# Retention, GLU and ReLU² in one kernel: v is scaled behind the state copy in the lone stage, conversions stand behind a pair's outputs, raw pieces are requested one by one, and k, v go ahead of the GLU blocks

## The chip, the core and the metric

The kernel runs on one core of a Trainium2 chip. The metric is the device time of the whole program in microseconds, the median over runs. The engines are TensorE (PE in the profile, PEld for its weight loads), VectorE (DVE), ScalarE (ACT), GpSimd (POOL) and SyncE (SP), which here only issues DMA requests. Each engine works through its own instructions in the order in which they were emitted, and waits on semaphores of the others.

## What is computed

Three stages follow one another. The first is a retention layer for 4 batches and 8 heads, without a softmax; its output, with the heads put side by side, is x of 2304 tokens by 512. The second is a gated linear unit behind an RMS norm, the third a ReLU² layer.

```python
ret = (q @ k.T) / sqrt(64) * where(i >= j, gamma_h ** (i - j), 0)   # 576 x 576 per head
x   = ret @ v                                                      # -> 2304 x 512
xn  = x / sqrt(mean(x * x) + 1e-6) * rms_g
y   = (silu(xn @ w_gate) * (xn @ w_val)) @ w_out                    # 512 -> 1536 -> 512
out = maximum(y @ w_in, 0) ** 2 @ w_out2                            # 512 -> 2048 -> 512
```

The weights come in as 8-byte numbers and are turned into fp32 on the chip.

## The kernel before

**Retention.** The 32 heads are taken in 16 pairs n = 0 to 15 (two heads fill the 128 partitions). A sequence of 576 positions is cut into four chunks of 128 and a rest of 64. For each pair TensorE makes, in this order: the scores `s` of the chunks (L354), `inner(n - 1)`, which multiplies the masked scores `ret` of the pair before by v into `o` (L418), the states `u` = kᵀv of the chunks (`state(n)`, L386), the rest's scores `r`, and `cross(n - 1)`, which adds the earlier chunks' states times q to `o` (L430, L436). Around it VectorE masks the scores (L357), ScalarE copies the states out of PSUM into `R` (L395), VectorE sums `R` over the chunks (L397) and writes `o` into the big buffer X (L447). A new `o` needs one of two PSUM banks that the `o` before has left, so `inner` waits for L447.

**Scaling v.** Before it is used, v of a pair is multiplied in place by per-row factors: `scale_v` (L346), two ScalarE operations, called for pair n + 1 at the end of the loop's turn for pair n. `inner` and `state` of that pair need it.

**Two stages of pairs.** Turns n = 1 to 7 are the lone stage (`alone`): only retention runs on TensorE, beside row sums, roots and scalings of the norm for the first 512 tokens (`beside`, told off by the table `NORMS`: `part` and `last` square X, `sum` makes the row sums `ssq` on TensorE, L522, `roots` makes the inverse roots on GpSimd, L458 to L466, `scale` spreads them by matmuls `rms`, L534). From n = 8 on each turn also calls `block()` twice, which does GLU matmuls `pg` and `pv` (L561 to L563) for the first 512 tokens with the weight pieces that are ready: the mixed stage.

**Weight pieces.** A raw piece (512 KB) is requested into one of three buffers (`load_piece`, L108), then converted (`convert_piece`): VectorE clamps it (`raw`, L134), ScalarE makes `u` and changes `raw` (L137, L139), VectorE joins them (L140), and `split` writes a rounded half by ScalarE (`w`, L158) and the remainder (L159), for the first two pieces on GpSimd. The raw buffer is free behind L140. `CONVERT` says at the end of which turn a piece is converted outside of a block, `LOAD_W` at which turns one more raw piece may be under way (`ahead`), and `CONVERT_BEHIND` behind which last instruction of ScalarE (`a`) and VectorE (`d`) a conversion is to stand, for each `phase` (0 up to n = 6, 2 from n = 7, 1 from n = 9).

**Requests.** TensorE's and SyncE's orders are as the code is written. k and v of pair n + 2 are requested (L286, L287) behind `state(n)`: at once in the lone stage, at the end of the turn (`load_late("kv")`) in the mixed one. q and k transposed (`qk`) of pair n + 4 follow `cross(n - 1)` likewise. A request that must wait for its buffer holds up all requests behind it. The orders of ScalarE, VectorE and GpSimd are set by a scheduler with its own idea of times, within `issue_after` bounds.

Of the kernel before, what the change touches and what calls it, by code (L numbers as in the profile page):

```python
# [8 lines left out]
F32 = mybir.dt.float32  # L9
F32R = mybir.dt.float32r  # L10
AF = mybir.ActivationFunctionType
ALU = mybir.AluOpType
# [35 lines left out]
    (6, 2): [("scale", 0), ("split", 0)], (7, 2): [("scale", 1), ("split", 1)],  # L48
    (9, 4): [("squares", 2)], (11, 3): [("sum", 2), ("roots", (2,))], (13, 3): [("scale", 2)],
}  # L50
LOAD_W = (4, 6)
NPOOL = 2
CONVERT = {3: 2, 5: 2, 8: 2, 9: 2}
CONVERT_BEHIND = ("", "ad", "ad", "ad")
RSQRT_MAGIC = float(0x5F3759DF)
I32 = mybir.dt.int32
U32 = mybir.dt.uint32
# [4 lines left out]
def retention_then_glu_then_relu2(ctx: ExitStack, tc: tile.TileContext, qk, kv, w1, w2, g, cmask, cvs, cgi, cgc, cid, out):  # L62
    nc = tc.nc
# [36 lines left out]
    last_on = {}  # L100
    cv = {"load": 0, "done": 0, "half": 0, "lim": 0, "load_lim": NP1, "phase": 0, "ahead": 0, "early": False}

    def load_piece():
        i = cv["load"]
        if i >= cv["load_lim"]:
            return
        t = stage.tile([P, 512, 2], I32, tag="st", name=f"raw{i}")
        nc.sync.dma_start(out=t.rearrange("p n t -> p (n t)"), in_=src[i].bitcast(I32))  # L108
        raws[i] = t
        cv["load"] += 1  # L110

    def load_ahead(i):
        while cv["load"] < min(i + cv["ahead"], cv["load_lim"]):
            load_piece()

    def convert():
# [4 lines left out]
        with ExitStack() as behind:  # L121
            for e in CONVERT_BEHIND[cv["phase"]]:
                behind.enter_context(tc.issue_after(last_on[e].ins))
            if "clamp" in last_on and not CONVERT_BEHIND[cv["phase"]]:
                behind.enter_context(tc.issue_after(last_on["clamp"].ins))
# [30 lines left out]

    def split(hi, lo, x, aside=nc.vector):
        nc.scalar.activation(out=hi, in_=x, func=AF.Copy)  # L158
        aside.tensor_tensor(out=lo, in0=x, in1=hi.bitcast(F32), op=ALU.subtract)  # L159

    first, saved, groups = {}, {}, {}
    L, R = slice(0, 2 * P), slice(2 * P, 4 * P)
# [80 lines left out]
    def halves(k):  # L243
        cv["half"] += k
        while cv["half"] >= 2 and convert():
            cv["half"] -= 2
        cv["half"] = min(cv["half"], 2)
# [6 lines left out]
    aside = wa.tile([P, 2, 512], F32, tag="w", name="aside")  # L254
# [8 lines left out]
    alone = {"on": True}  # L263
# [13 lines left out]
    def load_kv(n):  # L277
        if n >= NPAIR:
            return
        if n > 1:  # L280
            raw_k[n] = kvp.tile([P, 4, P], F32, tag="k", name=f"k{n}")
            v = ap.tile([P, 4 * P + D], F32, tag="v", name=f"v{n}", bufs=4)
        else:
            t = X[:, 2 + n, :8 * P + D]
            raw_k[n], v = t[:, :4 * P].rearrange("p (c n) -> p c n", c=4), t[:, 4 * P:]
        nc.sync.dma_start(out=raw_k[n], in_=kv[n][:, :4 * P].rearrange("p (c n) -> p c n", c=4))  # L286
        nc.sync.dma_start(out=v, in_=kv[n][:, 4 * P:])  # L287
        vsc[n], tails[n] = v[:, :4 * P].rearrange("p (c n) -> p c n", c=4), v[:, 4 * P:]
# [3 lines left out]
    def load_late(what):  # L292
        for n in late[what]:
            (load_kv if what == "kv" else load_qk)(n)
        late[what] = []
# [18 lines left out]
    for hp in range(HP):  # L314
        for h in (2 * hp, 2 * hp + 1):
            nc.gpsimd.tensor_scalar(
                out=mask[:, h], in0=causal[:, :C], scalar1=(1.0 - 2.0 ** (-5.0 - h)) ** -C, scalar2=None, op0=ALU.mult
            )
        nc.gpsimd.tensor_scalar(
            out=mask4[:, hp], in0=causal[:, C:], scalar1=vs[:, H + hp:H + hp + 1], scalar2=None, op0=ALU.mult  # L320
# [8 lines left out]
    for n in (2, 3):  # L329
        load_qk(n)  # L330
        load_kv(n)
    cv["ahead"] += 1
    load_ahead(0)
    for t, a in ((gsb, g), (ident, cid)):
        nc.sync.dma_start(out=t, in_=a)

    def scale_v(n):
        if n >= NPAIR:
            return
        hp = n % HP  # L340
        with ExitStack() as behind:
            if not alone["on"]:
                behind.enter_context(tc.issue_after(last_on["R"].ins))
            for h in range(2):
                r = slice(h * D, h * D + D)
                last_on["a"] = nc.scalar.activation(  # L346
                    out=vsc[n][:, :, r], in_=vsc[n][:, :, r], func=AF.Copy, scale=vs[:, 2 * hp + h:2 * hp + h + 1]
                )
# [13 lines left out]
    def scores(n, first=0, last=4):  # L362
        if not first:
            rets[n] = ap.tile([P, 2, 4 * C], F32, tag="ret", name=f"ret{n}")
        cols, h0 = slice(0, (last - first) * C), n % HP * 2
        if first:
            ps = [bank("V", f"s{n}_{h}")[:, None, cols] for h in range(2)]
        else:
            t = bank2("A0", f"s{n}")
            ps = [t[:, h:h + 1, cols] for h in range(2)]  # L370
        for c in range(first, last):
            for h in range(2):
                score(ps[h][:, 0, (c - first) * C:(c - first) * C + C], n, c, h, C)
        to = rets[n][:, :, first * C:last * C]
        if first:
            for h in range(2):
                masked(n, to[:, h:h + 1], ps[h], slice(h0 + h, h0 + h + 1), last - first)
        else:
            masked(n, to, t[:, :, cols], slice(h0, h0 + 2), last)
# [22 lines left out]
    def rest(n):  # L402
        ps = bank("A1", f"r{n}")
        for h, r in enumerate(both):
            score(ps[r, :REM], n, 4, h, REM)
        rets4[n] = ap.tile([P, REM], F32, tag="ret4", name=f"ret4_{n}")
        last_on["d"] = nc.vector.tensor_tensor(out=rets4[n], in0=ps[:, :REM], in1=mask4[:, n % HP], op=ALU.mult)
# [3 lines left out]
    def inner(n):  # L411
        ret = rets.pop(n)
        for half, chunks in enumerate(CHUNKS):
            po = pos[n, half] = bank("V", f"o{n}_{half}")
            for c in chunks[:2]:
                o = (c - 2 * half) * C
                for h, r in enumerate(both):
                    nc.tensor.matmul(  # L418
                        po[r, o:o + C], vsc[n][:, c, r], ret[:, h, c * C:c * C + C],
                        start=c == chunks[0], stop=False, skip_group_check=True,  # L420
                    )
# [31 lines left out]
    def roots(y, z, ms, sums, aside=False):  # L453

        last_on["d"] = nc.vector.tensor_scalar(
            out=ms, in0=sums, scalar1=1.0 / DM, scalar2=1e-6, op0=ALU.mult, op1=ALU.add
        )
        (nc.gpsimd if aside else nc.vector).tensor_scalar(  # L458
            out=y.bitcast(I32), in0=ms.bitcast(I32), scalar1=-0.5, scalar2=RSQRT_MAGIC, op0=ALU.mult, op1=ALU.add
        )  # L460
        for _ in range(3):
            if aside:
                nc.gpsimd.tensor_tensor(out=z, in0=y, in1=y, op=ALU.mult)
                nc.gpsimd.tensor_tensor(out=z, in0=z, in1=ms, op=ALU.mult)
                nc.gpsimd.tensor_scalar(out=z, in0=z, scalar1=-0.5, scalar2=1.5, op0=ALU.mult, op1=ALU.add)
                nc.gpsimd.tensor_tensor(out=y, in0=y, in1=z, op=ALU.mult)  # L466
                continue
            for o, a, c, op0, b, op1 in (
                (z, y, -0.5, ALU.mult, y, ALU.mult), (z, z, 1.0, ALU.mult, ms, ALU.mult), (y, z, 1.5, ALU.add, y, ALU.mult),
            ):  # L470
                last_on["d"] = nc.vector.scalar_tensor_tensor(out=o, in0=a, scalar=c, in1=b, op0=op0, op1=op1)
# [167 lines left out]


    scale_v(0)
    scores(0, 0, 2)
    keep_warm(WARM[1])
# [19 lines left out]
    def stages(n, at):  # L663
        with tc.high_priority():
            for what, i in NORMS.get((n, at), ()):
                beside(what, i)

    for n in range(1, NPAIR + 1):
        mixed = n > FIRST
        if n in LOAD_W:  # L670
            cv["ahead"] += 1
            load_ahead(cv["done"])
        if n == FIRST + 1:
            alone["on"] = False
        if n == FIRST:
            cv["phase"] = 2
        if n == FIRST + 2:
            cv["phase"] = 1
        if n < NPAIR:
            scores(n)  # L680
            stages(n, 0)
        inner(n - 1)
        if n < NPAIR:
            state(n)
            if n == NPAIR - 1:
                att_kv.close()
                wpool["c"] = glu.enter_context(tc.tile_pool(name="wc", bufs=NWC, side="right", reuse_waits="tile"))
                cv["lim"] = NGV + NWC
                cv["load_lim"] = NP1
                load_ahead(cv["done"])  # L690
        stages(n, 1)
        if n < NPAIR:
            rest(n)
        cross(n - 1)
        stages(n, 2)
        for i in range(2 * mixed):
            block()
            stages(n, 3 + i)
        load_late("kv")
        load_late("qk")  # L700
        scale_v(n + 1)
        halves(CONVERT.get(n, 0))
    need(NGV)
# [415 lines left out]
```

## Time and profile before

| | us |
|---|---|
| runs without a profile | 890.88, 890.40, 886.64; median 890.4 |
| profiled execution, whole | 895.79 |
| its span, first to last instruction | 894.0 |
| TensorE busy in the span | 879.6 (98%) |
| VectorE, ScalarE, GpSimd busy | 547.1, 422.9, 37.8 |
| HBM traffic | 142.5 MB read, 34.1 MB written |

Read it so: TensorE is busy nearly all the time, so what can be won is the 14.4 us in which it idles, and stretches in which it is busy at a lower clock. Its granted clock is printed as a share of 2.4 GHz, so 0.50 is the level of 1.2 GHz and a matmul takes twice as long in it. The retention stages lie in the first 140 us or so; the lone stage ends at 54.6 us, where the first `pg` stands.

### The profile page before, as it was taken

Reading aid. Unit: us, or ns where it says so; the run is one execution under the profiler, and the core shown is the slowest. Engines: PE = TensorE matmul, PEld = TensorE weight load, DVE = VectorE, ACT = ScalarE, POOL = GpSimd, SP = SyncE. Lnnn points to the kernel's source line nnn. Section 1 sums busy time; section 2 is a strip of 40 time slices with the busy share of each in tenths; the row PEclk is TensorE's granted clock in tenths of the full one; section 3 lists DMA queues with packets and bytes.
Section 4 is the critical chain, followed back from the end, with each engine's and each line's share of the span. In section 5 each row is a group of like instructions: output and inputs, shape, how many; then the busy total and the mean of one; then the engine's idle time right before and its main releaser. Section 6 shows DMA issues by size and latency. Waiting matters only on the chain.

```text
span 894.0 us, 13928 instructions
## 1 busy us (share of the span) xinstructions
PE 879.6 (98%) x5398; PEld 800.3 (90%) x5398; DVE 547.1 (61%) x935; ACT 422.9 (47%) x724; POOL 37.8 (4%) x70
## 2 busy tenths in 40 slices
PE   8899899999999999999999999999999999999998
PEld 7887788999988888888888889999999999999998
DVE  4567467656647665775664545359744498543864
ACT  3356445663333445344543434456635456344642
POOL 3320100001000000110000000000000000000000
PEclk9799899999999999999999999999999999999999
DMA  9746544321023545446568763469679587697701
GB/s 328 262 139 238 199 160 159 118 95 48 1 90 109 191 173 204 141 131 213 175 210 273 286 232 129 158 207 386 240 289 407 204 281 273 230 395 254 245 19 54
DMA packets 70643, 177.53 MB, mean 199 GB/s; under 512 B 7088, under 2 KB 27824, under 8 KB 70576
## 3 DMA queue, kind: packets, MB, share of 16 engines
q1 hardware_dynamic: 70144, 176.52, 56.3%
q8 instruction: 43, 0.70, 0.3%
q14 instruction: 24, 0.20, 0.1%
q10 hardware_dynamic: 432, 0.11, 0.1%
HBM read 142.52 MB, written 34.08 MB: 198 GB/s over the span
## 4 chain that ended last, share of the span: by engine, by line
PE 94%; DMA 4%; DVE 1%; SPq 1%; ACT 0%; issue 0%
PE b_M L562 7%; PE b_M L561 7%; PE b_M L563 7%; PE pg L561 6%; PE a L562 6%; PE a L561 6%; PE a L563 6%; PE pg L562 5%; PE pg L563 5%; PE pv L561 5%; PE pv L563 5%; PE pv L562 5%; PE m L561 4%; PE m L562 4%; PE m L563 4%; DMA v<-in_kv 3%
## 5 line engine op out<-in xcount | busy, mean ns | idle before, releaser
L563 PE MATMUL b_M<-hs_M,qr_oM 128*128 128x384 f32 x336 | 112.2, 334 | 0.0
L561 PE MATMUL b_M<-hs_M,qr_oM 128*128 128x384 f32 x336 | 112.2, 334 | 0.0
L562 PE MATMUL b_M<-hs_M,qr_oM 128*128 128x384 f32 x336 | 112.2, 334 | 0.0
L140 DVE SCALAR_TENSOR_TENSOR u<-u,raw 128x512 int32<-128x512 int32 x68 | 47.7, 704 | 70.7 <-ACT raw L139 70.6
L561 PE MATMUL pv<-xh,w 128*128 128x512 f32 (+1 forms) x240 | 90.0, 375 | 0.0
L561 PE MATMUL pg<-xh,w 128*128 128x512 f32 (+1 forms) x240 | 89.5, 373 | 0.0
L562 PE MATMUL pg<-xl,w 128*128 128x512 f32 (+1 forms) x240 | 88.8, 370 | 0.0
L563 PE MATMUL pg<-xh,w 128*128 128x512 f32 (+1 forms) x240 | 88.6, 369 | 0.0
L562 PE MATMUL a<-h,w 128*128 128x512 f32 (+1 forms) x240 | 88.6, 369 | 0.0
L561 PE MATMUL a<-h,w 128*128 128x512 f32 (+1 forms) x240 | 88.5, 369 | 0.0
L563 PE MATMUL pv<-xh,w 128*128 128x512 f32 (+1 forms) x240 | 88.4, 368 | 0.0
L563 PE MATMUL a<-h,w 128*128 128x512 f32 (+1 forms) x240 | 88.4, 368 | 0.0
L562 PE MATMUL pv<-xl,w 128*128 128x512 f32 (+1 forms) x240 | 88.3, 368 | 0.0
L137 ACT ACTIVATE u<-raw 128x512 f32<-128x512 f32 x68 | 45.2, 665 | 46.2 <-DVE raw L134 34.1
L590 ACT ACTIVATE h<-X 128x512 fp32r<-128x512 f32 (+1 forms) x52 | 30.2, 581 | 70.3 <-DVE X L609 44.8
L561 PEld LDWEIGHTS b_M<-hs_M,qr_oM 128*128 128x128 f32 x336 | 63.1, 188 | 0.0
L562 PEld LDWEIGHTS b_M<-hs_M,qr_oM 128*128 128x128 f32 x336 | 63.1, 188 | 0.0
L563 PEld LDWEIGHTS b_M<-hs_M,qr_oM 128*128 128x128 f32 x336 | 63.1, 188 | 0.0
L601 ACT ACTIVATE X<-pg 128x512 f32<-128x512 f32 (+1 forms) x52 | 28.2, 542 | 62.8 <-PE pg L563 62.7
L561 PEld LDWEIGHTS pg<-xh,w 128*128 128x128 f32 x240 | 45.5, 190 | 7.9
L563 PEld LDWEIGHTS pg<-xh,w 128*128 128x128 f32 x240 | 45.5, 190 | 7.7
L561 PEld LDWEIGHTS pv<-xh,w 128*128 128x128 f32 x240 | 45.2, 188 | 7.9
(183 smaller groups left out, 1895.1 us busy)
## 6 DMA issues: line engine op xcount, KB each, us to landing
qr<-s SPq DMA_DIRECT2D x84, 512.0 KB, 6.7
qr_oM<-soM SPq DMA_DIRECT2D x84, 512.0 KB, 6.3
raw<-in_w SPq DMA_DIRECT2D x68, 512.0 KB, 4.4
soM<-raw SPq DMA_DIRECT2D x32, 256.0 KB, 2.6
X<-in_qk SPq DMA_DIRECT2D x11, 576.0 KB, 6.4
s<-raw SPq DMA_DIRECT2D x8, 512.0 KB, 2.6
s<-raw SPq DMA_DIRECT2D x16, 256.0 KB, 3.7
s<-u SPq DMA_DIRECT2D x16, 256.0 KB, 4.9
```

Source lines behind the costliest of these rows:

```text
L137: scaled = nc.scalar.activation(out=u.bitcast(F32), in_=hf, func=AF.Prelu, scale=2.0 ** -112, alpha=-2.0 ** 32)
L140: nc.vector.scalar_tensor_tensor(out=u, in0=u, scalar=3, in1=low, op0=ALU.logical_shift_left, op1=ALU.bitwise_or)
L561: nc.tensor.matmul(dst, whi, xhi, start=start, stop=False, skip_group_check=True)
L562: nc.tensor.matmul(dst, whi, xlo, start=False, stop=False, skip_group_check=True)
L563: nc.tensor.matmul(dst, wlo, xhi, start=False, stop=stop, skip_group_check=True)
L590: last_on["a"] = nc.scalar.activation(out=h[:, 0, :n], in_=s, func=AF.Copy)
L601: last_on["a"] = nc.scalar.activation(out=s, in_=pg[:, :n], func=AF.Silu)
```

## The change

Seven edits go together. `scale_v` stands behind the last state copy `R` in the lone stage too, and no longer in the mixed stage alone. A conversion in phase 0 stands behind the last ScalarE and VectorE instructions of its turn (`"ad"`). The first conversion is made at turn 4 in place of 3. The first raw piece is no longer requested ahead of the loop but at turn 2, and one more may be under way from turns 4 and 7 on (it was 4 and 6). The GpSimd half of a split that comes after the roots stands behind them. In the mixed stage k and v are requested ahead of the two blocks, and qk behind the first.

```diff
-LOAD_W = (4, 6)
+LOAD_W = (2, 4, 7)
 NPOOL = 2
-CONVERT = {3: 2, 5: 2, 8: 2, 9: 2}
-CONVERT_BEHIND = ("", "ad", "ad", "ad")
+CONVERT = {4: 2, 5: 2, 8: 2, 9: 2}
+CONVERT_BEHIND = ("ad", "ad", "ad", "ad")
...
     def split(hi, lo, x, aside=nc.vector):
         nc.scalar.activation(out=hi, in_=x, func=AF.Copy)
-        aside.tensor_tensor(out=lo, in0=x, in1=hi.bitcast(F32), op=ALU.subtract)
+        with ExitStack() as behind:
+            if aside is nc.gpsimd and "root" in last_on:
+                behind.enter_context(tc.issue_after(last_on["root"].ins))
+            aside.tensor_tensor(out=lo, in0=x, in1=hi.bitcast(F32), op=ALU.subtract)
...
-    cv["ahead"] += 1
-    load_ahead(0)
...
-            if not alone["on"]:
+            if "R" in last_on:
                 behind.enter_context(tc.issue_after(last_on["R"].ins))
...
-                nc.gpsimd.tensor_tensor(out=y, in0=y, in1=z, op=ALU.mult)
+                last_on["root"] = nc.gpsimd.tensor_tensor(out=y, in0=y, in1=z, op=ALU.mult)
...
         stages(n, 2)
+        load_late("kv")
         for i in range(2 * mixed):
             block()
             stages(n, 3 + i)
-        load_late("kv")
+            load_late("qk")
         load_late("qk")
         scale_v(n + 1)
```

TensorE's instructions stand in the same order in both kernels. What moves on the others is shown at three places; numbers behind a name's letters are the pair or the piece.

ScalarE before, in the lone stage between the state copies R3 and R5 (`v` rows are `scale_v`, `R` rows state copies, `sq` squares for the norm, `u`, `raw` and `w` rows a conversion):

```order
L503 ACTIVATE sq0_355<-X_85 128x768
L503 ACTIVATE sq1_359<-X_85 128x768
L158 ACTIVATE w0_372<-u0_365 128x512
L346 ACTIVATE v5_330<-v5_330,vs_90 128x4x64 x2
L395 ACTIVATE R4_411<-u4_398 128x192
L508 ACTIVATE sq0_355<-X_85 128x256
L137 ACTIVATE u1_518<-raw1_370 128x512
L139 ACTIVATE raw1_370<-raw1_370 128x512
L508 ACTIVATE sq1_359<-X_85 128x256
L158 ACTIVATE w1_525<-u1_518 128x512
L346 ACTIVATE v6_408<-v6_408,vs_90 128x4x64 x2
L395 ACTIVATE R5_471<-u5_458 128x192
```

The same place in the changed kernel:

```order
L396 ACTIVATE R4_401<-u4_388 128x192
L347 ACTIVATE v5_330<-v5_330,vs_90 128x4x64 x2
L509 ACTIVATE sq0_355<-X_85 128x256
L509 ACTIVATE sq1_359<-X_85 128x256
L137 ACTIVATE u0_427<-raw0_239 128x512
L139 ACTIVATE raw0_239<-raw0_239 128x512
L396 ACTIVATE R5_471<-u5_458 128x192
L347 ACTIVATE v6_398<-v6_398,vs_90 128x4x64 x2
L158 ACTIVATE w0_434<-u0_427 128x512
L137 ACTIVATE u1_518<-raw1_365 128x512
L139 ACTIVATE raw1_365<-raw1_365 128x512
L158 ACTIVATE w1_525<-u1_518 128x512
```

Each state copy now comes ahead of the scaling of the next pair's v (R4 ahead of v5, R5 ahead of v6, and R2 ahead of v3, R7 ahead of v8 likewise), and the first piece's `w0` has come to stand behind the scaling of v6.

VectorE before, in the lone stage where piece 1 is clamped (`X` rows write `o` of a pair's two halves):

```order
L397 SCALAR_TENSOR_TENSOR R4_411<-R4_411,gc_93,u4_398 128x192
L447 TENSOR_TENSOR X_85<-o3_0_388,gi_92 128x256
L397 SCALAR_TENSOR_TENSOR R4_411<-R4_411,gc_93 128x128
L134 TENSOR_SCALAR raw1_370<-raw1_370 128x512
L447 TENSOR_TENSOR X_85<-o3_1_393,gi_92 128x320
L140 SCALAR_TENSOR_TENSOR u1_518<-u1_518,raw1_370 128x512
L357 TENSOR_TENSOR ret5_437<-s5_438,mask_89 128x1024
```

The same place in the changed kernel:

```order
L398 SCALAR_TENSOR_TENSOR R4_401<-R4_401,gc_93,u4_388 128x192
L448 TENSOR_TENSOR X_85<-o3_0_378,gi_92 128x256
L398 SCALAR_TENSOR_TENSOR R4_401<-R4_401,gc_93 128x128
L448 TENSOR_TENSOR X_85<-o3_1_383,gi_92 128x320
L134 TENSOR_SCALAR raw0_239<-raw0_239 128x512
L358 TENSOR_TENSOR ret5_437<-s5_438,mask_89 128x1024
L140 SCALAR_TENSOR_TENSOR u0_427<-u0_427,raw0_239 128x512
```

The clamp of a raw piece no longer stands between the two writes of X, and it is piece 0, not 1, that is clamped there. On GpSimd the remainder of piece 0 stays ahead of the roots, and that of piece 1 goes from ahead of them to behind.

SyncE before, requests of the mixed stage from the end of turn 8 to turn 10:

```order
L275 DMA qk11_781<-in_qk 128x1152
L108 DMA raw7_790<-in_w1 128x1024
L108 DMA raw8_865<-in_w1 128x1024
L108 DMA raw9_889<-in_w1 128x1024
L286 DMA k11_898<-in_kv 128x512
L287 DMA v11_899<-in_kv 128x576
L275 DMA X_85<-in_qk 128x2x576
L108 DMA raw10_910<-in_w1 128x1024
L108 DMA raw11_986<-in_w1 128x1024
L108 DMA raw12_1010<-in_w1 128x1024
L286 DMA k12_1015<-in_kv 128x512
L287 DMA v12_1016<-in_kv 128x576
```

The same requests in the changed kernel:

```order
L278 DMA qk11_757<-in_qk 128x1152
L108 DMA raw6_778<-in_w1 128x1024
L108 DMA raw7_790<-in_w1 128x1024
L289 DMA k11_846<-in_kv 128x512
L290 DMA v11_847<-in_kv 128x576
L108 DMA raw8_869<-in_w1 128x1024
L278 DMA X_85<-in_qk 128x2x576
L108 DMA raw9_894<-in_w1 128x1024
L108 DMA raw10_910<-in_w1 128x1024
L289 DMA k12_966<-in_kv 128x512
L290 DMA v12_967<-in_kv 128x576
```

k and v of pairs 11 and 12 are now requested two raw pieces earlier: v11 behind raw7 and not raw9, v12 behind raw10 and not raw12.

## Rows read from the trace of the kernel before

**Rows 1.** TensorE in order of time: start, duration, [idle before, releaser].

```profile
12.56 1.16 PE L354 MATMUL s<-X 64*128 64x128 f32 x16
16.29 1.16 PE L354 MATMUL s<-X 64*128 64x128 f32 x16
...
19.91 0.66 PE L418 MATMUL o<-ret,v 128*64 128x128 f32 x8 [1.87 <-DVE X L447]
...
22.65 1.16 PE L354 MATMUL s<-X 64*128 64x128 f32 x16 [0.47 <-DVE ret L357]
...
30.09 1.12 PE L418 MATMUL o<-ret,v 128*64 128x128 f32 x8 [1.96 <-DVE X L447]
...
50.40 1.93 PE L418 MATMUL o<-ret,v 128*64 128x128 f32 x16 [1.68 <-DVE X L447]
...
95.76 1.51 PE L386 MATMUL u<-v,k 128*64 128x64 f32 x16 [3.09 <-ACT v L346]
```

**Rows 2.** Stretches: us, busy of each engine, PEclk (granted clock), DMA share, GB/s.

```profile
30.00:40.30 10.30, 10.21 (x88) 9.74 (x90) 4.50 (x10) 3.73 (x9) 3.86 (x14) 0.50 0.48 168
...
50.50:53.90 3.40, 3.40 (x42) 3.15 (x44) 3.40 (x8) 2.18 (x6) 2.67 (x5) 0.50 0.09 34
...
94.90:101.70 6.80, 5.94 (x46) 5.11 (x47) 4.81 (x10) 3.40 (x7) 0.00 (x0) 0.50 0.25 82
...
112.00:894.00 782.00, 778.39 (x4256) 712.68 (x4252) 481.20 (x797) 369.89 (x618) 13.97 (x12) 1.00 0.55 194
```

**Rows 3.** ScalarE in order of time, the lone stage.

```profile
17.55 0.91 ACT L346 ACTIVATE v<-v,vs 128x256 f32<-128x256 f32 x2 [3.24 <-DMA v<-in_kv]
18.36 0.31 ACT L395 ACTIVATE R<-u 128x192 f32<-128x192 f32 x1
...
22.02 0.91 ACT L346 ACTIVATE v<-v,vs 128x256 f32<-128x256 f32 x2 [1.28 <-DMA v<-in_kv]
...
24.77 0.61 ACT L158 ACTIVATE w<-u 128x512 fp32r<-128x512 f32 x1
...
47.22 0.91 ACT L346 ACTIVATE v<-v,vs 128x256 f32<-128x256 f32 x2 [5.31 <-DMA v<-in_kv]
48.03 1.32 ACT L544 ACTIVATE xh<-X 128x256 fp32r<-128x256 f32 x4
49.26 0.31 ACT L395 ACTIVATE R<-u 128x192 f32<-128x192 f32 x1
```

**Rows 4.** VectorE in order of time, the clamp of piece 1.

```profile
29.20 0.43 DVE L134 TENSOR_SCALAR raw<-raw 128x512 f32<-128x512 f32 x1 [1.48 <-DMA raw<-in_w]
29.55 0.48 DVE L447 TENSOR_TENSOR X<-o,gi 128x320 f32<-128x320 f32 x1
```

**Rows 5.** SyncE's queue in order of time, turn 10: raw requests, then v.

```profile
81.35 5.24 SPq L108 DMA_DIRECT2D raw<-in_w  x3
...
87.11 0.43 SPq L287 DMA_DIRECT2D v<-in_kv  x1
```

**Rows 6.** The chain that ended last: a transfer from its request to its landing.

```profile
87.11 8.07 DMA v<-in_kv
```

**Rows 7.** TensorE: the row sums of the first 512 tokens.

```profile
31.99 3.57 PE L522 MATMUL ssq<-ones,sq 128*128 128x1 f32 x16
```

**Rows 8.** DMA traffic of one stretch of the lone stage (columns as in rows 2).

```profile
25.00:30.00 5.00, 3.13 (x59) 2.63 (x54) 2.69 (x7) 2.15 (x6) 3.31 (x4) 1.00 0.98 336
```

**Rows 9.** GpSimd in order of time: piece 1's remainder, the roots' first and last, a later root.

```profile
32.35 1.28 POOL L159 TENSOR_TENSOR w<-u,w 128x512 fp32r<-128x512 f32 x1 [4.04 <-ACT w L158]
35.86 0.19 POOL L458 TENSOR_SCALAR aside<-aside 128x4 int32<-128x4 int32 x1 [2.23 <-DVE aside L455]
...
39.23 0.20 POOL L466 TENSOR_TENSOR aside<-aside 128x4 f32<-128x4 f32 x1
...
89.73 0.74 POOL L463 TENSOR_TENSOR aside<-aside 128x2 f32<-128x2 f32 x1
```

**Rows 10.** VectorE beside that later root.

```profile
89.72 0.69 DVE L140 SCALAR_TENSOR_TENSOR u<-u,raw 128x512 int32<-128x512 int32 x1 [0.43 <-ACT raw L139]
```

## Prediction

> **What bounds it now.** I looked first at TensorE in order of time, for its idle time, since it is the engine that is busy nearly throughout. Five idle stretches of the retention stages carry nearly all of what it idles there [rows 1]: 1.87, 0.47, 1.96 and 1.68 us in the lone stage, together 5.98, and 3.09 us in the mixed stage, for the scaled v of pair 12. The reader is to see who ends each: VectorE's write of X or its masking four times, ScalarE's scaling of v once. Then I read the stretches for the granted clock [rows 2]: it stands at 0.50, which is 1.2 GHz, in three places ahead of 112 us, and TensorE is busy in them for 10.21, 3.40 and 5.94 us. Work in them takes twice as long, so they cost 5.1, 1.7 and 3.0 us. Each begins in or just behind an idle stretch: 28.1 to 30.1, 48.7 to 50.4, 92.7 to 95.8. The idle stretch before 19.91 was as long as two of these and no fall followed, so three of these four long idle stretches were followed by a fall. Behind 112 us TensorE is busy for 778.39 of 782 us at the full clock [rows 2], so nothing that the change does there can matter much: all that can be won lies in the first 112 us, and it is 5.98 + 3.09 + 9.8 = 18.9 us.
>
> **Why the lone stage idles.** ScalarE shows it [rows 3]. At 17.55 it scales v3, the moment it has landed, after 3.24 us of idle time, and only behind that, at 18.36, copies the state R2, whose `u` has been ready for some 3 us (the pair began at 12.56 [rows 1]). VectorE's sums of R2 and its writes of X follow, and `inner` waits for the bank. The same at 47.22: v8 is waited for over 5.31 us, `xh` follows, and R7 comes at 49.26. The wait that ends at 30.09 has another cause: VectorE's clamp of raw piece 1 waits 1.48 us for that piece's landing, and the write of X stands right behind it [rows 4].
>
> **The change, part by part.**
>
> State copies ahead of v: R2 ahead of v3 and R7 ahead of v8 take away the 1.87, most of the 0.47 (VectorE was late from the first wait and from piece 0's conversion, which also moves later) and the 1.68. Gain 4.0 us.
>
> Conversions behind the outputs, and later: piece 1's clamp no longer stands ahead of a write of X, and piece 0, which stands there now behind both writes, is requested at turn 2 and so has landed long before. Gain 1.96 us.
>
> What is late next? TensorE runs into landings and into GpSimd. I let it run on at its undisturbed pace: one pair takes 16.29 - 12.56 = 3.73 us [rows 1], of which scores and `inner` are about 2.1.
> - State 3 is wanted at 18.4; v3 is scaled at 17.55 + 0.91 = 18.46 [rows 3]. It waits some 0.15 us.
> - State 4 is then wanted at 22.2; v4 lands at 22.0 and is scaled at 22.93 [rows 3]. Moving raw piece 0 behind qk4 does not help v4, as the piece's 512 KB still stand ahead of it. It waits 0.75 us.
> - `rms`, behind `cross` of pair 5, needs the roots. Pair 5's scores start at 16.29 + 2 x 3.73 + 0.9 = 24.65. The row sums took 3.57 us at half clock [rows 7], so 1.8 at full; then `rms` is wanted at 24.65 + 2 x 3.73 + 1.8 = 33.9. On GpSimd the roots stand behind piece 0's remainder, that behind `w0` on ScalarE, and `w0` now behind the scaling of v6. Between v4 and v6 qk5, k5, v5, qk6, raw 1, k6 and v6 are to land, 2752 KB by their shapes, or 2176 KB when qk5 has landed by then; at 336 GB/s [rows 8] that is 8.4 or 6.6 us, so v6 lands at 28.7 to 30.4; I take 29.5. Add 0.91 for the scaling and 0.61 for `w0` [rows 3], 1.28 for the remainder and 39.43 - 35.86 = 3.57 for the roots [rows 9]: 35.9. TensorE waits about 2.0 us, with bounds of 0 (TensorE itself later by then) and 3.
>
> One more row bears on these roots: a root of 0.20 us took 0.74 at 89.73 [rows 9], while VectorE ran an operation of 0.69 us with two SBUF operands from 89.72 [rows 10]. The Trainium skill (SBUF — State Buffer, "Who interferes with whom") says why: a VectorE instruction with two inputs in SBUF and a GpSimd instruction that reads SBUF exclude each other for the whole of the one that came first. These two rows agree with it: 0.54 us longer. By that rule piece 1's conversion beside the roots would lengthen them by about 0.5 us, and the sum would be 0.5 us higher; I leave it inside the bounds of that wait.
>
> So the lone stage's idle time goes from 5.98 to some 2.9. Its clock: without the idle stretches ahead of them the falls at 30.0 and 50.5 should not come, a gain of 5.1 + 1.7 = 6.8 us. But the new wait at `rms` is as long as those that brought falls in three of four cases, so in the likeliest case one fall stays; I price it at the shortest in the trace, 3.40 us, which is 1.7 us, since steady work follows it.
>
> k, v ahead of the blocks: SyncE's three raw requests in turn 10 took from 81.35 to 86.6, as each waits for a buffer that a conversion must leave, and v12 was requested only at 87.11 [rows 5] and took 8.07 us [rows 6], landing at 95.18; its scaling and TensorE's wait to 95.76 followed. In the new order v12 stands behind the first of these three requests. It goes out at about 82.2 in the old time, lands by 90.3 even if it took the same 8.07 us, and is scaled by 91.2, ahead of 92.7 where TensorE was ready. The 3.09 us go, and with them the fall behind them, 3.0 us. The cover is about 1.5 us at worst; v11, requested two raw pieces earlier, has more. Raw pieces now stand behind k and v: at worst 544 KB, 1.7 us at 336 GB/s [rows 8], and the traffic beside the stall is only 82 GB/s [rows 2], so I price that at nothing. qk behind the first block moves by one block, for pairs three turns on: nothing.
>
> **The sum**, against the profiled execution: 895.8 - 5.98 - 3.09 - 9.8 + 2.9 + 1.7 = 881.5 us. That execution was 5.4 us over the median of the runs, 890.4, and those three differ by 4.2 us among themselves, which is as much as one or two falls of the clock are worth. If the runs had fewer falls, the change has less to take from them; if profiling only adds time, all of the gain carries over. I take the middle, half of the 5.4: 878.8, say 879.
>
> **Rivals.**
> - The lone stage keeps its falls of the clock, because the `rms` wait and the row sums are enough for long ones; the waits go as above. 895.8 - 5.98 - 3.09 - 3.0 + 2.9 = 886.6, less 2.7: 884. For it speaks that three of four such waits brought a fall and that one lasted 10.3 us over the row sums; against it that the wait at `rms` comes behind those.
> - No new wait: the roots come in time and no fall is left. 895.8 - 18.9 = 876.9, less 2.7 to 5.4: 871.5 to 874. It needs v6 to land by 27.5, for which 336 GB/s is too little.
> - The lone stage is bound by landings: at a DMA share of 0.98 [rows 8] each wait removed comes back as one for v or qk, and its falls too. Then only the mixed stage gains: 895.8 - 6.1 - 2.7 = 887, no change. Against it: one pair's 1120 KB take 3.4 us at 336 GB/s, less than the pair's 3.73; only the raw pieces push it over.
> - Slower: in the mixed stage raw pieces, now behind k, v and one by one, land up to 1.7 us later, and `pg` waits for its converted piece in every turn. With a short fall behind each wait a turn costs 3.4 us. The gain of 14.3 is used up from a little over four of eight turns on; in all eight the time is 881.5 + 27 - 2.7 = 906. Against it: no row shows TensorE waiting for a piece, and raw requests wait for buffers, not for the traffic.
>
> **Chances and range.** My forecast 0.62, no new wait 0.10, falls kept 0.15, bound by landings 0.08, slower 0.05. The three runs of before span 0.5%, about what a measurement of this kernel can tell from no change; 0.5% below the median is 886. Forecast, no new wait and two thirds of falls kept are below it: faster 0.82; the rest of falls kept and the landings are the same: 0.13; slower 0.05. The range runs from 869 (no new wait with the whole 5.4 off and a mixed stage a little tighter) to 888 (the landings' case with its bound), and leaves out the slower case and the tails.
>
> **What would show it.** Right: TensorE's waits at 19.9, 30.1 and 50.4 gone, the state copies at most 0.5 us behind their `u`; the first `pg` some 8 us earlier than 54.6; v12's scaling with no TensorE wait behind it; 1.00 as granted clock from there on. A new wait of 1 to 3 us at `rms` near 34 us, ended by the roots on GpSimd, and a short stretch at 0.50 behind it. Wrong: waits of `s` or `state` for landings in each pair, a stretch at 0.50 of 7 us or more in the lone stage, or TensorE waiting for the remainder of a weight piece (L162) in the mixed stage. If the runs gain much less than the profiled execution, the middle that I took between the two was wrong.

## The result, and the profile after

The changed kernel takes 878.34 us (median of 6 runs, 878.09 to 879.38), against 890.14 us of before in the same measurement (886.64 to 892.72): a ratio of 0.9872, with a 95% interval of 0.9851 to 0.9893. Its profiled execution took 878.09 us, with a span of 876.3.

The head of its page, the span and what TensorE was busy for:

```profile
span 876.3 us, 13929 instructions
...
PE 869.8 (99%) x5398; PEld 792.1 (90%) x5398; DVE 548.3 (63%) x935; ACT 423.8 (48%) x724; POOL 38.5 (4%) x70
```

Against 894.0 and 879.6 of before, 17.7 us are gone in the profiled pair: 9.8 us of busy time, which is the same matmuls without the low clock (half of the 19.6 us in [rows 2]), and 7.9 us of TensorE's idle time, 14.4 to 6.5.

Three stretches of the changed kernel, lone stage, mixed stage up to 112 us and the rest, with the columns of [rows 2]:

```profile
3.00:44.90 41.90, 39.99 (x655) 35.97 (x654) 30.11 (x63) 19.85 (x47) 19.80 (x40) 1.00 0.99 360
44.90:112.00 67.10, 67.10 (x646) 56.09 (x644) 49.78 (x104) 40.78 (x77) 4.55 (x15) 1.00 0.62 213
112.00:876.30 764.30, 760.71 (x4100) 698.09 (x4098) 468.20 (x768) 361.67 (x601) 13.95 (x12) 1.00 0.55 194
```

The granted clock is 1.00 in all three. TensorE idles 1.9 us in the lone stage and not at all up to 112 us; behind it, 3.6 us as before.

TensorE in order of time, answering to [rows 1]:

```profile
12.61 1.16 PE L355 MATMUL s<-X 64*128 64x128 f32 x16
...
16.40 1.16 PE L355 MATMUL s<-X 64*128 64x128 f32 x16
17.50 1.09 PE L419 MATMUL o<-ret,v 128*64 128x128 f32 x16
18.42 0.98 PE L387 MATMUL u<-v,k 128*64 128x64 f32 x16
...
22.79 1.08 PE L387 MATMUL u<-v,k 128*64 128x64 f32 x16
23.80 0.33 PE L355 MATMUL r<-X 64*64 64x64 f32 x4
...
27.75 1.95 PE L523 MATMUL ssq<-ones,sq 128*128 128x1 f32 x16
...
36.24 0.71 PE L535 MATMUL rms<-aside 128*128 128x128 f32 x4 [1.66 <-POOL aside L467]
...
44.98 0.50 PE L562 MATMUL pg<-xh,w 128*128 128x512 f32 x1
...
81.37 0.63 PE L387 MATMUL u<-v,k 128*64 128x64 f32 x16
```

`inner` at 17.50 runs through, with no wait for X. States 3 and 4 (18.42 and 22.79) take 0.98 and 1.08 us where an undisturbed one, that at 81.37, takes 0.63: their v was scaled while they stood there. One wait has brackets, the 1.66 us for the roots. The first `pg` starts 9.6 us earlier than before, and state 12, at 81.37, waits for nothing.

ScalarE in the lone stage, answering to [rows 3]:

```profile
17.77 0.91 ACT L347 ACTIVATE v<-v,vs 128x256 f32<-128x256 f32 x2 [2.08 <-DMA v<-in_kv]
19.49 0.33 ACT L396 ACTIVATE R<-u 128x192 f32<-128x192 f32 x1 [0.82 <-ACT v L347]
22.23 0.91 ACT L347 ACTIVATE v<-v,vs 128x256 f32<-128x256 f32 x2 [2.40 <-DMA v<-in_kv]
...
24.51 0.30 ACT L396 ACTIVATE R<-u 128x192 f32<-128x192 f32 x1
...
29.36 0.91 ACT L347 ACTIVATE v<-v,vs 128x256 f32<-128x256 f32 x2 [0.74 <-DMA v<-in_kv]
30.18 0.61 ACT L158 ACTIVATE w<-u 128x512 fp32r<-128x512 f32 x1
...
35.01 0.31 ACT L396 ACTIVATE R<-u 128x192 f32<-128x192 f32 x1
```

R3 is copied at 19.49, as soon as its `u` is there. R4 (24.51) comes 0.6 us behind its `u`, as squares stand ahead of it, and R6 (35.01) 1.6 us behind, as the conversion of piece 1 does. The forecast had named 0.5 us as the most. TensorE shows no idle time behind the first, and behind the second it waited for the roots anyway.

GpSimd, answering to [rows 9]:

```profile
30.87 1.27 POOL L162 TENSOR_TENSOR w<-u,w 128x512 fp32r<-128x512 f32 x1 [4.04 <-ACT w L158]
32.22 0.25 POOL L459 TENSOR_SCALAR aside<-aside 128x4 int32<-128x4 int32 x1
...
33.96 0.54 POOL L465 TENSOR_TENSOR aside<-aside 128x4 f32<-128x4 f32 x1
...
35.99 0.20 POOL L467 TENSOR_TENSOR aside<-aside 128x4 f32<-128x4 f32 x1
36.14 1.27 POOL L162 TENSOR_TENSOR w<-u,w 128x512 fp32r<-128x512 f32 x1
```

This is the chain behind the 1.66 us, link by link: v6 lands and is scaled at 29.36, `w0` follows at 30.18, its remainder on GpSimd at 30.87, then the roots from 32.22 to 36.19, and `rms` at 36.24. It shows the order of events; that the remainder is what holds `rms` is tested below.

SyncE's queue where v12 is requested, answering to [rows 5]:

```profile
63.55 6.14 SPq L108 DMA_DIRECT2D raw<-in_w  x2
69.73 0.43 SPq L289 DMA_DIRECT2D k<-in_kv  x1
70.60 0.33 SPq L290 DMA_DIRECT2D v<-in_kv  x1
```

Raw requests still hold up the queue for 6 us, but v12 goes out at 70.60, 10.8 us ahead of state 12. Before it was 5.6 us (87.11 against 92.67).

### The profile page after: what moved, and what is told of

Same layout as the page of the kernel before. It is cut to its first block, busy times and chain, and to the rows that moved or that the text cites. A ratio compares the mean times of both kernels' runs of the same rounds, so it can differ in the third digit from the quotient of the medians.

```text
span 876.3 us, 13929 instructions
## 1 busy us (share of the span) xinstructions
PE 869.8 (99%) x5398; PEld 792.1 (90%) x5398; DVE 548.3 (63%) x935; ACT 423.8 (48%) x724; POOL 38.5 (4%) x70
## 4 chain that ended last, share of the span: by engine, by line
PE 95%; DMA 2%; SPq 1%; POOL 0%; ACT 0%; issue 0%; DVE 0%
PE b_M L564 7%; PE b_M L563 7%; PE b_M L562 7%; PE pg L562 6%; PE pv L562 6%; PE a L563 6%; PE a L562 6%; PE pv L564 6%; PE a L564 6%; PE pg L563 6%; PE pv L563 6%; PE pg L564 6%; PE m L564 4%; PE m L563 4%; PE m L562 4%; PE q L564 2%
## 5 line engine op out<-in xcount | busy, mean ns | idle before, releaser
L140 DVE SCALAR_TENSOR_TENSOR u<-u,raw 128x512 int32<-128x512 int32 x68 | 47.7, 705 | 64.6 <-ACT raw L139 64.5
L134 DVE TENSOR_SCALAR raw<-raw 128x512 f32<-128x512 f32 x68 | 29.2, 436 | 38.4 <-DMA raw<-in_w 32.8
L562 PEld LDWEIGHTS pv<-xh,w 128*128 128x128 f32 x240 | 45.2, 188 | 7.9
L564 PEld LDWEIGHTS pv<-xh,w 128*128 128x128 f32 x240 | 45.2, 188 | 7.7
```

The lines of the kernel that those rows point to most:

```text
L134: last_on["clamp"] = nc.vector.tensor_scalar(out=hf, in0=hf, scalar1=-MAG_MAX, scalar2=MAG_MAX, op0=ALU.max, op1=ALU.min)
L140: nc.vector.scalar_tensor_tensor(out=u, in0=u, scalar=3, in1=low, op0=ALU.logical_shift_left, op1=ALU.bitwise_or)
L562: nc.tensor.matmul(dst, whi, xhi, start=start, stop=False, skip_group_check=True)
L564: nc.tensor.matmul(dst, wlo, xhi, start=False, stop=stop, skip_group_check=True)
```

## The experiments

The baseline moves between runs, as the clock falls in it in some and not in others, so each kernel is given with the median of before beside it.

**Each edit alone.** The kernel before, with one of the three parts.

v alone:

```diff
-            if not alone["on"]:
+            if "R" in last_on:
```

> The kernel before with one edit: v is scaled behind the state copy in the lone stage. Theory A (waits and the falls behind them go part by part): the waits of TensorE that ended at 19.9 and 50.4 us (1.87 and 1.68 us) go, and the short fall behind the second; the wait for raw piece 1's clamp (1.96 us) and the mixed stage's 3.09 us stay, with their falls. Some 4 us of idle time less, 884 to 887 us. Theory B (the lone stage is bound by landings or by the other edit): each wait comes back a pair later, 889 to 891 us. If falls of the granted clock do not hang on the waits (theory C), stretches at 0.50 appear where TensorE did not idle.

The conversion edits alone (the remainder behind the roots too, as in the change's diff):

```diff
-LOAD_W = (4, 6)
+LOAD_W = (2, 4, 7)
-CONVERT = {3: 2, 5: 2, 8: 2, 9: 2}
-CONVERT_BEHIND = ("", "ad", "ad", "ad")
+CONVERT = {4: 2, 5: 2, 8: 2, 9: 2}
+CONVERT_BEHIND = ("ad", "ad", "ad", "ad")
-    cv["ahead"] += 1
-    load_ahead(0)
```

> The kernel before with the conversion edits alone: first piece requested at turn 2, converted at turn 4, both pieces behind a turn's outputs, piece 1's remainder behind the roots. Theory A: the 1.96 us wait at 30.1 us goes, and perhaps the fall behind it; those for state copies behind v (1.87, 1.68) and the mixed stage's 3.09 us stay: 885 to 888 us. Theory B: no gain without the edit on v, as the state copy still waits for v's landing: 889 to 891 us.

k, v ahead of the blocks alone:

```diff
+        load_late("kv")
         for i in range(2 * mixed):
             block()
             stages(n, 3 + i)
-        load_late("kv")
+            load_late("qk")
```

> The kernel before with k, v requested ahead of the blocks alone. Theory A: v12 is requested some 5 us earlier in its turn, TensorE's 3.09 us wait at state 12 goes and with it the 6.8 us at 0.50 behind it: 3.1 to 6.1 us less, 884 to 887 us; the lone stage is as before. Rival: raw pieces, now behind k and v, are late, and TensorE waits for a remainder (L159) in the mixed stage: 890 us or more.

Measured, beside 889.47 us of before (885.04 to 892.7): v alone 885.91 (ratio 0.9963, 0.9939 to 0.9988), conversions alone 886.12 (0.9962, 0.9942 to 0.9981), k, v alone 885.60 (0.9958, 0.9939 to 0.9977). These are 3.6, 3.4 and 3.9 us, together 10.8, and the whole change brought 11.8. So alone the parts are of about one size, within intervals of some 2 us to each side, and each time lies in the range of its theory A.

Their traces show whose wait went, and that not every edit clears its waits alone. With v alone the clamp's wait stays, and the long fall right at its end; TensorE in order of time, and then the stretch with the columns of [rows 2]:

```profile
20.62 0.66 PE L418 MATMUL o<-ret,v 128*64 128x128 f32 x8 [1.01 <-DVE X L447]
...
31.32 0.72 PE L418 MATMUL o<-ret,v 128*64 128x128 f32 x8 [2.48 <-DVE X L447]
```

```profile
31.80:42.00 10.20, 10.20 (x92) 9.73 (x90) 5.34 (x9) 2.27 (x6) 3.85 (x14) 0.50 0.50 167
```

The wait near 20 us did not go as expected: 1.01 of its 1.87 us are left. VectorE in order of time shows that the clamp of piece 0 also stood ahead of that write of X, and waited for the piece's landing:

```profile
19.74 0.43 DVE L134 TENSOR_SCALAR raw<-raw 128x512 f32<-128x512 f32 x1 [1.49 <-DMA raw<-in_w]
20.08 0.48 DVE L447 TENSOR_TENSOR X<-o,gi 128x320 f32<-128x320 f32 x1
```

So that wait had two causes, and it takes the edit on v and the conversion edits together to end it. In the mixed stage TensorE waited 0.97 us for v12 in this execution, and no fall followed, though k, v were requested as before.

With the conversions alone, TensorE in order of time shows waits for X of the old kind, and two stretches have a low clock:

```profile
20.07 0.66 PE L419 MATMUL o<-ret,v 128*64 128x128 f32 x8 [1.62 <-DVE X L448]
24.49 0.66 PE L419 MATMUL o<-ret,v 128*64 128x128 f32 x8 [0.47 <-DVE X L448]
35.43 1.09 PE L419 MATMUL o<-ret,v 128*64 128x128 f32 x16 [1.97 <-DVE X L448]
```

```profile
36.60:43.40 6.80, 5.93 (x60) 5.17 (x56) 4.30 (x10) 4.37 (x10) 4.02 (x13) 0.50 0.77 254
91.20:94.60 3.40, 3.40 (x22) 2.80 (x19) 3.40 (x8) 1.23 (x3) 0.00 (x0) 0.50 0.16 51
```

The clamp's wait went, but one of the same length came 5 us later: the state copy R5 stood behind the scaling of v6, whose landing ScalarE awaited for 3.11 us. The second stretch follows a wait of 2.34 us for v12.

With k, v alone the lone stage keeps waits of 1.46, 2.79 and 1.57 us and its long fall, while in the mixed stage no wait of TensorE above 0.15 us and no fall is left.

**All but one edit.** The changed kernel with one part undone, each the reverse of a diff above.

> The changed kernel without the edit on v. If the parts add up: the 3.5 us that this edit took alone come back, 881 to 883 us, with TensorE's waits for X of 1 to 2 us near 20 and 35 to 50 us and a fall or two of the clock behind them. If the parts share their gain, under 880 us.

> The changed kernel without the conversion edits. If the parts add up: 881 to 883 us, with the wait for X near 31 us behind a raw piece's clamp and a fall behind it. If the parts share their gain, under 880 us.

> The changed kernel without k, v ahead of the blocks. If the parts add up: 881 to 884 us, all of it in the mixed stage, with a wait of 1 to 3 us for v12 near 80 us; the lone stage is that of the changed kernel, with rms waiting 1.66 us and no fall. If v12 comes in time once the lone stage is faster, about 878.5 us.

Measured: without v 880.53 us (880.26 to 881.76), without the conversions 884.03 (882.59 to 886.29), without k, v 881.61 (880.26 to 882.91), beside 887.49 of before. Against 878.34 of the whole change they cost 2.2, 5.7 and 3.3 us, 11.2 together; against 879.12, which the changed kernel took in a later measurement, each is 0.8 us less. The sum holds, the single parts do not: v's edit missed its 881 to 883 from below, and the conversions' passed theirs. The conversion edits, worth 3.4 us alone, are worth 5.7 beside the others; v's edit, worth 3.6 alone, 2.2. Without the conversion edits the clamp's wait is 2.38 us and a fall of 6.8 us follows; without v's edit TensorE still waits for X (1.21, 0.48, 0.49 us) and for the roots (2.07 us), but in that profiled execution no fall came.

Without k, v the profiled execution has two falls, with the columns of [rows 2]:

```profile
29.70:33.10 3.40, 3.40 (x38) 3.28 (x34) 1.48 (x5) 1.65 (x4) 2.11 (x5) 0.50 0.83 275
84.30:87.70 3.40, 3.19 (x36) 2.96 (x38) 2.29 (x3) 2.41 (x6) 0.00 (x0) 0.50 0.06 25
```

The second stands at TensorE's wait of 2.48 us for v12 (ended at 84.51). The first has no idle time ahead of it: what TensorE did before it fell was the row sums, from 27.54 to 29.49. `rms` did not wait in this execution, so the expected 1.66 us with no fall turned into a fall with no wait. So theory C of the first expectation is right in part: falls follow long waits, but not each one, and this one came without any, as did another below.

**Roots ahead of the remainders, first way.** Conversions one turn later, so that the roots come first.

```diff
-CONVERT = {4: 2, 5: 2, 8: 2, 9: 2}
+CONVERT = {5: 2, 6: 2, 8: 2, 9: 2}
```

> The changed kernel with the first two pieces converted at turns 5 and 6 instead of 4 and 5, so that on GpSimd the roots stand ahead of both remainders. Theory A (the 1.66 us that TensorE waits at rms come from piece 0's remainder, which stands behind v6's scaling on ScalarE): the wait at rms goes to under 0.3 us and the time falls by 1.3 to 1.7 us to about 876.9 us. Rival: VectorE, late with the masking and the sums of R6 behind a conversion, holds TensorE at the same place anyway, at the scores of pair 7 or at inner: 878 to 878.6 us.

It took 880.56 us (880.32 to 881.85): 2.2 us more than the changed kernel, and neither theory had that. The wait at `rms` did go, but one for VectorE came, a pair later than my rival had placed it. Its VectorE, and then its TensorE, in order of time:

```profile
39.30 0.45 DVE L134 TENSOR_SCALAR raw<-raw 128x512 f32<-128x512 f32 x1
41.06 1.20 DVE L140 SCALAR_TENSOR_TENSOR u<-u,raw 128x512 int32<-128x512 int32 x1 [1.31 <-ACT raw L139]
42.18 1.21 DVE L358 TENSOR_TENSOR ret<-s,mask 128x1024 f32<-128x1024 f32 x1
```

```profile
43.45 1.16 PE L355 MATMUL s<-X 64*128 64x128 f32 x16 [2.37 <-DVE ret L358]
```

Piece 1's joining (L140) waits for ScalarE, the masking of pair 7 stands behind it, and the next pair's scores wait for the bank; a fall of 3.4 us follows.

**Second way: one instruction moved.** The changed kernel, with piece 0's remainder kept back until the roots have been emitted.

```diff
+        if aside is nc.gpsimd and "root" not in last_on:
+            later_low.append(low)
+        else:
+            low()
...
             roots(y, z, ms, parts["bank"][:, at], aside=True)
+            while later_low:
+                later_low.pop(0)()
```

> The changed kernel with one instruction moved: piece 0's remainder on GpSimd stands behind the roots, with no other order changed. Theory A (the 1.66 us at rms come from that remainder in GpSimd's queue): the roots start when the row sums are there, near 29.9 us, and end near 33.5, so rms does not wait; VectorE's clamp beside the remainder (1.12 us for 0.42) is quick again too; about 876.7 us. Rival, after the run with conversions at turns 5 and 6: VectorE's masking of pair 6, late behind piece 1's conversion, holds the scores of pair 7 in the place of rms: 0.4 to 1.2 us of the gain are lost, 877.0 to 878.0 us.

It took 876.94 us (876.8 to 878.18): 1.4 us under the changed kernel, as theory A had it. TensorE in order of time:

```profile
34.55 0.71 PE L544 MATMUL rms<-aside 128*128 128x128 f32 x4
35.20 1.16 PE L362 MATMUL s<-X 64*128 64x128 f32 x16
36.29 0.66 PE L426 MATMUL o<-ret,v 128*64 128x128 f32 x8
37.18 0.66 PE L426 MATMUL o<-ret,v 128*64 128x128 f32 x8 [0.24 <-DVE X L455]
```

`rms` no longer waits; the rival's wait for VectorE is there, but only 0.24 us long. Once more, on one chip with the changed kernel and a third variant:

> The changed kernel with piece 0's remainder behind the roots, once more: 876.8 to 877.5 us, 1.0 to 1.7 us under the changed kernel on the same chip. If its first gain was a matter of the chip, the two are within 0.4 us.

> The changed kernel once more, beside the two below on one chip. 878.0 to 879.4 us, with a granted clock over the span of 0.998 or more in every run; if falls of the clock come without a wait of TensorE, some runs show 0.996 to 0.997 and are 1.5 to 3 us longer.

> The changed kernel with q, k transposed requested at the end of the turn again, k, v still ahead of the blocks. If that half of the edit is worth nothing, as the prediction priced it: within 0.4 us of the changed kernel. Rival: qk lands late for the scores of a pair in the mixed stage, a wait there and 1 us or more.

The version with the roots first took 877.07 us (876.95 to 878.54), the changed kernel 879.12 (878.31 to 881.98), and the one with qk requested at the end of the turn 879.76 (878.50 to 880.85), beside 889.36 of before. So the first is 2.0 us faster than the changed kernel here, was 1.4 us under its first median before, and has the lowest median of all that ran. The changed kernel spread more than expected: its longest run, 881.98, has a mean clock of 0.998 like its shortest, so those 3.7 us are not the clock's. Of the qk half nothing can be told: the ranges lie within each other. Its trace has no wait for qk in the mixed stage; what made its profiled execution the slowest of its runs is in the lone stage, where the edit moves nothing: the scaling of v6 began at 30.66 and not 29.36, `rms` waited 3.09 us and not 1.66, and a fall followed:

```profile
38.00:41.40 3.40, 3.40 (x30) 3.00 (x30) 2.75 (x5) 1.59 (x4) 2.73 (x5) 0.50 0.71 282
```

The profiled execution of the changed kernel in this last measurement had a fall ahead of `rms`, with no wait of TensorE behind its row sums (27.64 to 29.59). TensorE in order of time, and the stretch of the fall:

```profile
36.44 0.71 PE L535 MATMUL rms<-aside 128*128 128x128 f32 x4 [0.38 <-POOL aside L467]
```

```profile
30.80:34.20 3.40, 3.40 (x32) 3.17 (x34) 2.10 (x3) 1.44 (x3) 2.54 (x8) 0.50 0.91 319
```

It took 878.31 us, 0.2 us more than the one without a fall, 878.09: nearly all that the fall costs, TensorE waits less at `rms`.

## Why the prediction was right

It said 879 and 878.34 came out, with the gain where it was placed. By its steps:

- State copies ahead of v, and conversions behind the outputs: right. The waits at 19.91, 30.09 and 50.40 [rows 1] are gone. Two things were read too simply. The wait at 19.91 was put down to R2 behind v3 alone; with v's edit alone 1.01 us of it stayed, for the clamp of piece 0, so the 4.0 us of that step needed the conversion edits too. And the copies R4 and R6 came later than the 0.5 us allowed, with no idle time of TensorE put down to them.
- The new waits: right in place and nearly in size. States 3 and 4 took 0.15 and 0.75 us in the forecast; their groups are 0.35 and 0.45 us longer than undisturbed, with 0.13 us of idle time ahead of state 4. `rms` was to wait 2.0 us and waited 1.66: it was wanted at 34.58 and not 33.9, and the roots ended at 36.19 and not 35.9. They took 3.97 us for 3.57, within the 0.5 us that were left inside the bounds. v6 was taken to land at 29.5 and its scaling started at 29.36, but that is luck in part: I took 336 GB/s and the middle of two amounts, and the changed kernel has, with the columns of [rows 2],

```profile
20.00:30.00 10.00, 9.81 (x158) 8.66 (x156) 7.55 (x16) 6.33 (x14) 2.88 (x4) 1.00 1.04 388
```

  At 388 GB/s the larger amount, 2752 KB, takes 7.3 us from 22.0. The one-instruction kernel shows the cause to be the remainder in GpSimd's queue, and the execution with v6 scaled at 30.66 fits a wait that follows v6's landing.
- k, v ahead of the blocks: right. v12 goes out 5.2 us earlier against state 12, as worked out (82.2 for 87.11), the wait and its fall are gone, and no raw piece is waited for.
- The one fall that was to stay, priced at 1.7 us: wrong for the first profiled execution, where none came. In two others the fall lay ahead of `rms`, and the wait there shrank to 0.38 us or went; I had added the whole wait and the fall. It stood where I had put it only once, behind the wait of 3.09 us.
- The forecast for a profiled execution, 881.5, was 3.4 us over 878.1. That fall is half of it, the rest is idle time. Before, with the columns of [rows 2]:

```profile
3.00:112.00 109.00, 99.24 (x1139) 85.67 (x1140) 65.68 (x137) 51.56 (x106) 23.65 (x54) 0.91 0.68 239
```

  TensorE idled 9.76 us there, and 1.91 after; I had it go from 9.07 to 2.9. So 0.7 us are small waits that I left out, and 1.0 us is what the new waits lack of 2.9, in part because the profile counts the longer groups of states 3 and 4 as busy.
- The way from the profiled execution to the median, half of 5.4 us: wrong as an argument. Nothing was to be taken off: the changed kernel's profiled execution, 878.09 us, is even the lowest of its six, 0.25 us under their median. The profiled execution of before was one with a poor clock, 0.988 on average over its span, where 54 runs of before beside the experiments have 0.990 to 0.998 and tend to be longer the lower it is (884.8 us at 0.997, 893.1 at 0.990, though the longest, 893.4, has 0.994). So the runs of before lost some 4 us to the clock, not 9.8. This is an estimate: the median's gain of 11.8 us less the 7.9 us of idle time, if the runs idled as long as the profiled execution; a mean clock of 0.995 over 887 us gives 4.4. The 2.7 us taken off and the 3.4 us of the line above are errors of opposite sign, and that 879 came so close to 878.34 is luck to that extent.

What stays open is what lets a wait of 1.2 to 2.5 us bring a fall in one place and none in another, and what lets one come without a wait.

## What to carry to other kernels

On an engine that works in order, an operation that waits for a transfer belongs behind everything whose inputs are already there, and one that releases a PSUM bank ahead of everything that may wait; the trace shows a breach of it as a short operation that starts right behind another engine's or a DMA's landing. A wait that is taken away uncovers the next one in the same chain, so it pays to run the undisturbed pace on by hand and ask at each step what is there in time: here that found the wait for the roots, and the one-instruction cure for it. Where a clock falls behind waits, one profiled execution shows one draw of it: weigh idle time and clock apart before a gain is carried over to the median.

## What the runs showed of the hardware

VectorE and GpSimd lengthen each other's operations. VectorE in the changed kernel, in order of time:

```profile
31.30 1.12 DVE L134 TENSOR_SCALAR raw<-raw 128x512 f32<-128x512 f32 x1
...
36.28 1.27 DVE L398 SCALAR_TENSOR_TENSOR R<-R,gc 128x128 f32<-128x128 f32 x1
```

They take 0.42 and 0.34 us elsewhere, and stand beside GpSimd's remainders, 30.87 to 32.14 and 36.14 to 37.41; each ends within 0.3 us of the remainder beside it. With the remainder moved, the clamp took 0.42 us again. The other way round, the root at 33.96 took 0.54 us for 0.20 beside VectorE's joining at 33.75. The Trainium skill (SBUF — State Buffer, "Who interferes with whom") has it as an exclusive lock on a pair of ports that the two share, held for a whole instruction, and these rows agree.

TensorE's granted clock fell to 0.50 behind row sums with no wait ahead of it in two executions (at 29.7 us without k, v ahead, at 30.8 us in the changed kernel), and not in others with the same row sums. A fall that ended in a wait for another engine cost 0.2 us (878.31 for 878.09).
